# A dilated causal convolution on one core: common parts split a second time in PSUM, and the last 16 channels gathered in DRAM

## The chip, the cores and the metric

One NeuronCore of one Trainium2 chip runs the whole kernel in a single launch. The metric is the device time of one execution in microseconds (us). Engines are named as in the profile: PE is TensorE (PEld its weight loads), ACT is ScalarE, DVE is VectorE, POOL is GpSimd, and SP is the engine that here only issues transfers.

## What is computed

The reference is one WaveNet layer: a causal convolution with 15 taps, dilation 2, 144 channels in and 288 out, a gate, and a projection of 144 by 144.

```
B, T, D, K = 2, 16000, 144, 15          # x: B,T,D   w: K,D,2D   w_o: D,D   (all bf16)
xp = pad(x, 28 zeros in front of T)
h  = sum over i of  xp[:, 28-2i : 28-2i+T, :] @ w[i]
f, g = h[..., :144], h[..., 144:]
return (tanh(f) * sigmoid(g)) @ w_o
```

## The kernel before

**Tiling.** Both sequences and a gap of 32 zero tokens form one line of 32032 tokens. It is cut into ten blocks of 3072 tokens and one of 1536. Even and odd tokens are two planes, so that dilation 2 becomes a step of 1 inside a plane. A block of 3072 has two units (r = 0 and 1), the last block has one: 21 units. In a unit each of 128 rows of a matmul result stands for 12 pairs of output positions.

**Fewer matmuls.** Taps are not multiplied one by one. A Karatsuba-like scheme (L129 and L135 to L183) makes sums and differences of shifted inputs on DVE: S, D, E of the input at a distance of 8, S4, D4, E4 of those at a distance of 4, and Sr, Dr, Er of the last 16 channels. Four parts m = 0 to 3 use (S, D, E, E). Each part has a common product V (`pe_V`, 8 matmuls: two banks of 4) and two private products A for b2 = 1 and 0 (`pe_A`, two banks of 4 matmuls plus 1 for the last 16 channels). A unit has 110 of these matmuls, each 128 by 128 against 288 columns, and from the second unit on 24 of 144 columns for the projection. ACT copies V and A of parts 0 and 1 out of PSUM as bf16 (L291), DVE adds them (L129), for parts 2 and 3 with the A operand read from PSUM. `gate_act` makes tanh and sigmoid on ACT (L306, L307), `gate_mul` their product z on DVE.

**The last 16 channels.** 144 channels do not fit 128 rows. `load_x` transposes channels 0 to 127 into `xn` and channels 16 to 143 into `xb`, two DMA transposes each (L117). `load_r` copies the last 16 rows of `xb` eight times, each shifted by one token, into `rx` (L125, 16 rows by 2 planes by about 1544 tokens each), so that one matmul covers eight taps of those channels.

**Projection and store.** `start_zT` transposes z by DMA (L318), `outproj` multiplies it with `w_o` one unit later (groups of 6 matmuls, ACT copies each group to `os`, L329), `store` writes `os` to the output (L348). In a 64-row store each packet is one token of 288 bytes.

**Order.** Every engine runs in program order, written out by hand and kept (`K_`). SP issues all steady transfers in order: in an odd unit zT, the four transposes of the block after next, the store; in an even unit zT, the eight copies to `rx`, the store. All SP transfers share one DMA queue (q1), ACT's are on q10, POOL's on q0.

**PSUM.** Three two-bank tiles `acc` and two one-bank tiles `po`, all eight banks.

Of the kernel before, what the change touches and what calls it, by code (L numbers as in the profile page):

```python
# [15 lines left out]
def kernel(  # L16
# [6 lines left out]
):  # L23

# [38 lines left out]
    v_pool = ctx.enter_context(tc.tile_pool(name="v", bufs=4))  # L63
# [3 lines left out]
    ps_acc = ctx.enter_context(tc.tile_pool(name="ps_acc", bufs=3, space=bass.MemoryType.PSUM))  # L67
    ps_out = ctx.enter_context(tc.tile_pool(name="ps_out", bufs=2, space=bass.MemoryType.PSUM))
# [34 lines left out]
    blocks = {}  # L103

    def load_x(bi, names=("xn", "xb")):
        loads, zeros = segs(bi)
        cur = blocks.setdefault(bi, dict(bi=bi))
        for nm in names:
            c0 = 0 if nm == "xn" else D - P
            t_ = xa_pool.tile([P, 2, XW], BF16, name=nm)  # L110
            cur[nm] = t_
            for (a, e) in zeros:
                K_(nc.gpsimd.memset(t_[:, :, a:e], 0.0))
            for e in range(2):
                for (col, b, tk, n) in loads:
                    src = bass.AP(x.tensor, x[b, tk + e, c0].offset, [[2 * D, n], [1, P]])
                    K_(nc.sync.dma_start_transpose(out=t_[:, e, col:col + n], in_=src))  # L117

    def load_r(bi, engs=None):
        engs = engs or (nc.sync,)  # L120
        cur = blocks[bi]
        cw = HA + BTOK[bi] // 2
        rx = xa_pool.tile([P, 2, XW], BF16, name="rx")
        for i in range(8):
            K_(engs[i % len(engs)].dma_start(out=rx[CR * i:CR * (i + 1), :, 8:cw], in_=cur["xb"][P - CR:P, :, 8 - i:cw - i]))  # L125
        cur["rx"] = rx

    def tt(out_, a, b, op):
# [4 lines left out]
           "Sr": (0, 8), "Dr": (0, 8), "Er": (-8, 16)}  # L133

    def derive(bi, nm):  # L135
        cur = blocks[bi]
        big = bi < NBIG
        npd = BTOK[bi] // 48
        u0, wd = GEO[nm]
        t_ = d_pool.tile([P, GEO[nm][1] * P], BF16, name=nm)  # L140
        cur[nm] = t_

        def src(x_, u):

            s = u + HA
            v = x_[:, :, s:s + PU * npd]
            if big and wd == PU:
                return v
            return v.rearrange("p e (k j) -> p e k j" if big else "p e (k j) -> p j e k", j=PU)[
                (slice(None),) * (3 if big else 1) + (slice(0, wd),)]  # L150

        if nm in ("S4", "D4", "E4"):
            b = cur[nm[0]]
            bw = GEO[nm[0]][1]
            if big:
                b3 = b[:].rearrange("p (n j) -> p n j", j=bw)
                tt(t_[:].rearrange("p (n j) -> p n j", j=wd), b3[:, :, 4:4 + wd], b3[:, :, 0:wd], ALU.subtract)
            else:
                rw = 2 * npd
                tt(t_[:, 0:wd * rw], b[:, 4 * rw:(4 + wd) * rw], b[:, 0:wd * rw], ALU.subtract)  # L160
            return
        x_ = cur["rx" if nm[-1] == "r" else "xn"]
        if big:
            o = t_[:].rearrange("p (e c) -> p e c", e=2) if wd == PU else \
                t_[:].rearrange("p (e k j) -> p e k j", e=2, j=wd)
        else:
            o = t_[:, 0:wd * 2 * npd].rearrange("p (j e k) -> p j e k", e=2, k=npd)
# [5 lines left out]
    def stat(cur, nm, u):  # L173

        u0, wd = GEO[nm]
        blk, r = cur["blk"], cur["r"]
        t_ = blk[nm]
        if r is None:
            rw = 2 * (BTOK[blk["bi"]] // 48)
            return t_[:, (u - u0) * rw:(u - u0 + 2) * rw]  # L180
        return t_[:].rearrange("p (n j) -> p n j", j=wd)[:, :, u - u0 + r]


    wz = const.tile([P, 512], BF16)
    K_(nc.vector.memset(wz[:], 0.0))
    w_all = const.tile([CM, K, D2], BF16)
    wrA = const.tile([P, D2], BF16)
    wrB = const.tile([P, D2], BF16)
    K_(nc.gpsimd.memset(wrB[96:P, :], 0.0))
    for (t0, t1) in ((0, 4), (4, 8), (8, 12), (12, K)):  # L190
        K_(nc.scalar.dma_start(out=w_all[:, t0:t1, :], in_=w[t0:t1, 0:CM, :].rearrange("k c d -> c k d")))
    warm = const.tile([P, 1], F32)
    K_(nc.gpsimd.memset(warm[:], 0.0))
    K_(nc.scalar.activation(out=warm[:], in_=warm[:], func=ACT.Sigmoid))
    load_x(0)
# [5 lines left out]
    ident = const.tile([P, P], BF16)  # L201
    make_identity(nc, ident[:])
    K_(nc.gpsimd.dma_start(out=wrA[:], in_=w[0:8, CM:D, :]))
    K_(nc.gpsimd.dma_start(out=wrB[0:7 * CR, :], in_=w[8:K, CM:D, :]))
    load_r(0, (nc.sync, nc.gpsimd))
    load_x(1)
# [7 lines left out]
    load_r(1, (nc.sync, nc.gpsimd))  # L214

    wps = ps_acc.tile([P, 2, 512], F32, name="acc")
    for _ in range(54):
        K_(nc.tensor.matmul(wps[:, 0, :], lhsT=wz[:, 0:P], rhs=wz[:], start=True, stop=True))

    G1 = const.tile([CM, 7, D2], BF16)  # L220
    Gm = const.tile([CM, 7, D2], BF16)
    H = const.tile([CM, 4, 4, D2], BF16)
    Wr = const.tile([P, 4, 2, D2], BF16)

    tt(H[:, 2], w_all[:, 0:4, :], w_all[:, 4:8, :], ALU.add)
    GO = ((G1, ALU.add), (Gm, ALU.subtract))
    for (g, op) in GO:
        tt(g[:, 0:4, :], w_all[:, 0:4, :], w_all[:, 8:12, :], op)
    for m, (g, op) in enumerate(GO):
        tt(g[:, 4:7, :], w_all[:, 4:7, :], w_all[:, 12:15, :], op)  # L230
        tt(H[:, m, 0:3, :], g[:, 0:3, :], g[:, 4:7, :], ALU.add)
        tt(H[:, m, 3, :], g[:, 3, :], w_all[:, 7, :], ALU.add)
    derive(0, "S")
    derive(0, "D")
    derive(0, "E")
    tt(H[:, 3, 0:3], w_all[:, 8:11, :], w_all[:, 12:15, :], ALU.add)
    derive(0, "S4")
    tt(Wr[:, 0, 1, :], wrA[:], wrB[:], ALU.add)
    tt(Wr[:, 1, 1, :], wrA[:], wrB[:], ALU.subtract)
    derive(0, "D4")  # L240
    derive(0, "Sr")
    derive(0, "Dr")
    derive(0, "E4")
    derive(0, "Er")
    K_(nc.scalar.copy(out=H[:, 3, 3, :], in_=w_all[:, 11, :]))
    for m in (2, 3):
        K_(nc.scalar.mul(out=Wr[:, m, 0, :], in_=(wrA[:], wrB[:])[m - 2], mul=-1.0))
    front_neg = [lambda m=m: K_(nc.scalar.mul(out=Wr[:, m, 0, :], in_=Wr[:, m, 1, :], mul=-1.0)) for m in range(2)]

    def Gw(m, i):  # L250
        j = i + 8 * (m - 2) if m >= 2 else i
        if m < 2 and i < 7:
            return (G1, Gm)[m][:, i, :]
        return w_all[:, j, :] if j < K else None

    def Rw(m, b2):
        return Wr[:, m, b2, :] if m < 2 or not b2 else (wrA, wrB)[m - 2][:]
# [4 lines left out]
    HALF = (0.5, 0.5, 1.0, 1.0)  # L262

    def mm_bank(ps, jobs):
        n = len(jobs)
        for k, (l, r) in enumerate(jobs):
            K_(nc.tensor.matmul(ps, lhsT=l, rhs=r, start=(k == 0), stop=(k == n - 1)))  # L267

    def pe_V(cur, m):
        acc = ps_acc.tile([P, 2, 512], F32, name="acc")  # L270
        for b1 in range(2):
            mm_bank(acc[:, b1, 0:D2], [(stat(cur, NM[m], SH[m] + 2 * b1 - i), H[:, m, i, :]) for i in range(4)])
        return acc

    def pe_A(cur, m, b2):
        acc = ps_acc.tile([P, 2, 512], F32, name="acc")
        for b1 in range(2):
            jobs = []
            for i in range(4):
                wt = Gw(m, i if b2 else i + 4)  # L280
                if wt is not None:
                    jobs.append((stat(cur, NM[m] + "4", SH[m] + 2 * b1 - i - (0 if b2 else 4)), wt))
            jobs.append((stat(cur, NM[m] + "r", SH[m] + 2 * b1 + 4 * b2), Rw(m, b2)))
            mm_bank(acc[:, b1, 0:D2], jobs)
        return acc
# [4 lines left out]
    def act_ev(dst, acc, sign=1.0):  # L290
        K_(nc.scalar.activation(out=dst, in_=acc[:, :, 0:D2], func=ACT.Copy, scale=sign))  # L291

    def ev_V(acc, m):
        v = v_pool.tile([P, 2, D2], BF16, name="v")
        act_ev(v[:], acc, HALF[m])
        return v

    def bc(v):
        v = v[:]
        return bass.AP(v.tensor, v.offset, [list(v.ap[0]), [0, 2]] + [list(p) for p in v.ap[1:]])  # L300

    def gate_act(cur, c0, n=4):
        th = g_pool.tile([P, 4, D], BF16, name="th")
        sg = g_pool.tile([P, 4, D], BF16, name="sg")
        y = cur["y"]
        K_(nc.scalar.activation(out=th[:, 0:n], in_=y[:, c0:c0 + n, 0:D], func=ACT.Tanh))  # L306
        K_(nc.scalar.activation(out=sg[:, 0:n], in_=y[:, c0:c0 + n, D:D2], func=ACT.Sigmoid))  # L307
        cur["g", c0] = (th, sg, n)

    def gate_mul(cur, c0):  # L310
        th, sg, n = cur["g", c0]
# [4 lines left out]
    def start_zT(cur):  # L316
        zT = zt_pool.tile([P, ZW // P, P], BF16, name="zT")
# [4 lines left out]
    def outproj(cur, g):  # L322
        po = ps_out.tile([P, 512], F32, name="po")
# [214 lines left out]
```

## Time and profile before

| what | value |
|---|---|
| median of 3 runs | 353.64 us (352.66 to 357.31) |
| profiled execution: own time | 354.34 us |
| profiled execution: span from first to last instruction | 352.6 us |
| mean granted TensorE clock | 0.989 |
| busy: PE, PEld, DVE, ACT | 95%, 90%, 83%, 63% |
| DMA | 141881 packets, 45.33 MB; q1 busy 73.6% of 16 engines |

Times in the trace count from the start of the span. A group of the profile is one line of code, engine, operation and shape, with its busy time and the mean of one in ns. An x288 matmul shows some 286 ns because the pipeline is filled and emptied in it; one starts every 0.122 us. The chain of waits follows the work that ended last from the end back to the start. The trace also holds each DMA packet with start, duration, size and queue.

### The profile page before, as it was taken

How to read it: one execution, taken by the hardware profiler on the slowest of the kernel's cores; microseconds unless marked ns; L12 is line 12 of the kernel's file. 1: busy time of each engine (PE TensorE's matmuls, PEld its weight loads, DVE VectorE, ACT ScalarE, POOL GpSimd, SP SyncE). 2: the span in 40 equal slices, each digit the busy share in tenths (PEclk: the TensorE clock that was granted, in tenths of full speed). 3: DMA queues.
4: the chain of work that ended last, by engine and by line, in shares of the span. 5: the costliest groups of instructions: out<-in, count | busy, mean ns of one | idle time of the engine just before them, and what ended most of it. 6: DMA issues, size and time to landing. Idle time of an engine off the chain costs nothing.

```text
span 352.6 us, 7171 instructions
## 1 busy us (share of the span) xinstructions
PE 334.4 (95%) x2891; PEld 318.0 (90%) x2892; DVE 293.2 (83%) x393; ACT 220.8 (63%) x388; POOL 21.3 (6%) x48
## 2 busy tenths in 40 slices
PE   8938899999999999989999999989999999999994
PEld 3527799999999999989999999989999999999873
DVE  1826999789889888977988897878889889979984
ACT  2122567576765767657576765757676575776773
POOL 5255100000000000000000000000000000000002
PEclk9987999999999999999999999999999999999999
DMA  9998899969869787697997888698789865633224
GB/s 203 132 119 181 89 157 148 120 131 180 129 97 196 145 91 145 110 162 110 196 151 94 161 122 137 86 187 168 92 169 159 121 116 90 121 73 60 59 46 93
DMA packets 141881, 45.33 MB, mean 129 GB/s; under 512 B 136938, under 2 KB 139306, under 8 KB 141848
## 3 DMA queue, kind: packets, MB, share of 16 engines
q1 hardware_dynamic: 138588, 42.28, 73.6%
q0 software_dynamic: 1024, 1.43, 3.1%
q10 hardware_dynamic: 2236, 1.17, 1.3%
q8 instruction: 22, 0.36, 0.4%
q14 instruction: 11, 0.09, 0.1%
HBM read 1.62 MB, written 9.22 MB: 31 GB/s over the span
## 4 chain that ended last, share of the span: by engine, by line
PE 83%; DMA 9%; SPq 3%; DVE 2%; POOL 1%; ACT 1%; issue 0%; ACTq 0%; POOLq 0%
PE acc L267 74%; PE po L267 9%; DMA zT<-z 6%; SPq L117 3%; DMA wo_ab<-in_w_o_dram 2%; DMA xb<-in_x_dram 1%; DVE y L129 1%; POOL rx L125 1%; DVE m L129 0%; POOL wo_ab L211 0%; POOL wo_ab L212 0%; PE acc L359 0%; DVE mm L129 0%; DVE u L129 0%; DVE Sr L129 0%
## 5 line engine op out<-in xcount | busy, mean ns | idle before, releaser
L267 PEld LDWEIGHTS <-E 128*128 128x128 bf16 x966 | 117.5, 144 | 2.8 <-issue 1.8
L267 PE MATMUL acc<-w_all,E 128*128 128x288 bf16 x630 | 101.3, 286 | 1.7 <-DVE y L129 1.7
L329 ACT CAST os<-po 128x432 bf16<-128x432 f32 x80 | 41.4, 517 | 59.6 <-PE po L267 59.5
L267 PEld LDWEIGHTS <-S 128*128 128x128 bf16 x504 | 62.7, 142 | 1.6
L291 ACT ACTIVATE v<-acc 128x576 bf16<-128x576 f32 x84 | 52.4, 649 | 18.4 <-PE acc L267 18.4
L267 PEld LDWEIGHTS <-D 128*128 128x128 bf16 x504 | 63.2, 141 | 0.6
L267 PE MATMUL acc<-G,S 128*128 128x288 bf16 x294 | 49.4, 291 | 0.0
L267 PE MATMUL acc<-Gm,D 128*128 128x288 bf16 x294 | 48.0, 286 | 0.0
L306 ACT ACTIVATE th<-y 128x576 bf16<-128x576 bf16 (+1 forms) x64 | 43.4, 678 | 4.9 <-DVE y L129 4.9
L267 PE MATMUL po<-wo_ab,zT 128*128 128x144 bf16 x480 | 43.1, 226 | 3.2 <-DMA zT<-z 3.2
L267 PE MATMUL acc<-H,E 128*128 128x288 bf16 x336 | 44.6, 286 | 0.0
L307 ACT ACTIVATE sg<-y 128x576 bf16<-128x576 bf16 (+1 forms) x64 | 43.0, 672 | 0.0
L291 ACT ACTIVATE mm<-acc 128x576 bf16<-128x576 f32 x42 | 27.4, 652 | 24.1 <-PE acc L267 24.1
L267 PEld LDWEIGHTS <-zT 128*128 128x128 bf16 x480 | 35.3, 98 | 6.2 <-DMA zT<-z 4.3
L129 DVE TENSOR_TENSOR y<-m,acc 128x576 bf16<-128x576 bf16 x42 | 31.3, 752 | 8.5 <-PE acc L267 8.1
L129 DVE TENSOR_TENSOR m<-m,v 128x1152 bf16<-128x1152 bf16 x42 | 31.7, 755 | 3.6 <-ACT m L291 1.5
L129 DVE TENSOR_TENSOR z<-th,sg 128x576 bf16<-128x576 bf16 (+1 forms) x64 | 28.8, 449 | 6.3 <-ACT sg L307 5.3
L291 ACT ACTIVATE m<-acc 128x576 bf16<-128x576 f32 x42 | 26.9, 654 | 9.5 <-PE acc L267 9.5
L129 DVE TENSOR_TENSOR y<-u,acc 128x576 bf16<-128x576 bf16 x42 | 31.4, 748 | 0.6 <-PE acc L267 0.5
L267 PE MATMUL acc<-Wr,Sr 128*128 128x288 bf16 x84 | 24.5, 292 | 7.1 <-DVE Sr L129 7.1
L129 DVE TENSOR_TENSOR mm<-mm,v 128x1152 bf16<-128x1152 bf16 x21 | 15.9, 758 | 16.3 <-ACT mm L291 16.2
L267 PEld LDWEIGHTS <-Er 128*128 128x128 bf16 x168 | 24.2, 144 | 0.2
(65 smaller groups left out, 396.3 us busy)
## 6 DMA issues: line engine op xcount, KB each, us to landing
out_dram<-os SPq DMA_DIRECT2D x36, 216.0 KB
rx<-xb SPq DMA_DIRECT2D x72, 96.5 KB
w_all<-in_w_dram ACTq DMA_DIRECT2D x3, 288.0 KB
rx<-xb POOLq DMA_DIRECT2D x8, 96.5 KB, 5.6
out_dram<-os SPq DMA_DIRECT2D x4, 168.8 KB
rx<-xb SPq DMA_DIRECT2D x8, 48.5 KB
xn<-in_x_dram SPq DMA_TRANSPOSE x24
xb<-in_x_dram SPq DMA_TRANSPOSE x24
```

Of the source, the lines that this page charges most:

```text
L117: K_(nc.sync.dma_start_transpose(out=t_[:, e, col:col + n], in_=src))
L125: K_(engs[i % len(engs)].dma_start(out=rx[CR * i:CR * (i + 1), :, 8:cw], in_=cur["xb"][P - CR:P, :, 8 - i:cw - i]))
L129: return K_(nc.vector.tensor_tensor(out=out_, in0=a, in1=b, op=op))
L267: K_(nc.tensor.matmul(ps, lhsT=l, rhs=r, start=(k == 0), stop=(k == n - 1)))
L291: K_(nc.scalar.activation(out=dst, in_=acc[:, :, 0:D2], func=ACT.Copy, scale=sign))
L306: K_(nc.scalar.activation(out=th[:, 0:n], in_=y[:, c0:c0 + n, 0:D], func=ACT.Tanh))
L307: K_(nc.scalar.activation(out=sg[:, 0:n], in_=y[:, c0:c0 + n, D:D2], func=ACT.Sigmoid))
L329: K_(nc.scalar.copy(out=cur["os"][:, 3 * g:3 * g + 3, :].rearrange("p a d -> p (a d)"), in_=po[:, 0:3 * D]))
```

## The change

The common product is split once more. For each part, a first matmul pair (`v_common`) with 2 weights writes bank 0 of a tile X. ACT copies bank 0 to bank 1 inside PSUM (`copy_b1`). PE adds 2 private matmuls to each bank (`v_private`, stationary operands S2, D2, E2, new differences at a distance of 2 made by DVE). ACT copies each bank to a one-bank tile Y (`copy_b2`). PE then adds the private products of b2 = 1 onto X and of b2 = 0 onto Y, without starting a new accumulation. V has 6 matmuls for 8, a unit 102 for 110. V is no longer copied out or added on DVE; two of the four evictions of parts 0 and 1 become halves (`use`). Work is written as 84 periods (21 units by 4 parts), with v_common two periods ahead and v_private one; the projection of a unit is spread over the two units behind it. PSUM is now two X tiles of two banks, three Y and one `po`.

For the last 16 channels, `xb` and its transposes and the eight shifted copies are gone. `gather_r` copies channels 128 to 143 of a block's tokens from x to a DRAM buffer `rs` (runs of 32 bytes); `load_r` reads it by two DMA transposes whose rows overlap: each row has 256 bytes and begins 32 bytes after the one before. At the start, weight sums of parts 2 and 3 are made on PE with an identity matrix and copied out by ACT, and the warm-up is shorter. At the end, the transposes of z are grouped by four.

```diff
-    ps_acc = ... bufs=3 (two banks each)     ps_out = ... bufs=2
+    ps_x = ... bufs=2 (two banks each)   ps_y = ... bufs=3   ps_o = ... bufs=1
+    def gather_r(bi, eng):
+        for (col, b, tk, n) in segs(bi)[0]:
+            src = bass.AP(x.tensor, x[b, tk, CM].offset, [[D, 2], [2 * D, n], [1, CR]])
+            K_(eng.dma_start(out=bass.AP(rs[bi].tensor, rs[bi][col, 0].offset, [[RW[bi] * CR, 2], [CR, n], [1, CR]]), in_=src))
     def load_r(bi):
-        for i in range(8):
-            K_(engs[i % len(engs)].dma_start(out=rx[CR * i:CR * (i + 1), :, 8:cw], in_=cur["xb"][P - CR:P, :, 8 - i:cw - i]))
+        for e in range(2):
+            src = bass.AP(rs[bi].tensor, rs[bi][e * n + 1, 0].offset, [[CR, n], [1, P]])
+            K_(nc.sync.dma_start_transpose(out=t_[:, e, 0:n], in_=src))
...
+    gather_r(0, nc.scalar)          # behind the four loads of w_all
+    load_x(0)
+    load_r(0)
...
+    gather_r(1, nc.sync)
+    load_x(1)
+    load_r(1)
...
     def pe_V(cur, m):
-        acc = ps_acc.tile([P, 2, 512], F32, name="acc")
-        for b1 in range(2):
-            mm_bank(acc[:, b1, 0:D2], [(stat(cur, NM[m], SH[m] + 2 * b1 - i), H[:, m, i, :]) for i in range(4)])
+        mm(ps[:, 0, 0:D2], [(stat(cur, NM[m], SH[m] - j), H[:, m, 4 + j, :]) for j in range(2)], True)
+    def pe_Vp(cur, ps, m, b1):
+        mm(ps[:, b1, 0:D2], [... 2 jobs of NM[m] + "2" ...], False)
+    def copy_b1(q):
+            K_(nc.scalar.copy(out=X[q][:, 1, 0:D2], in_=X[q][:, 0, 0:D2]))
+    def copy_b2(q, b1):
+            Y[q, b1] = y_bank()
+            K_(nc.scalar.copy(out=Y[q, b1][:, 0:D2], in_=X[q][:, b1, 0:D2]))
+    def use(q, b2, b1=None):
+        if m < 2:   # ACT: scaled(..., 0.5), 576 columns of X or 288 of Y
+        else:       # DVE: tt(y, P, X or Y), 576 or 288 columns
+    def loads(ui, k):
+        if r == 1 and k == 2 and bi + 2 < NBLK:
             load_x(bi + 2)
+            gather_r(bi + 2, nc.sync)
+        if r == 0 and k == 2 and 1 <= bi and bi + 1 < NBLK:
             load_r(bi + 1)
+    def period(q):
+        if m == 0:
+            gate_act(p1, 0, 0); fill(ui, "E", "S"); gate_mul(p1, 8)
+            fill(ui, "E2", "S2", "S4", "D"); ... derive(bi, "Dr") ...; fill(ui, "E4")
+        if m == 1:
+            gate_mul(p1, 0); start_zT(p1)
...
+        pe_A(cur, X[q][:, 0, 0:D2], m, 1, 0, part)
+        pe_A(cur, X[q][:, 1, 0:D2], m, 1, 1, part)
+        v_private(q + 1)
+        use(q, 1)
+        copy_b2(q + 1, 0)
+        if m == 1:
+            both(cur, 1); fill(ui, "Er", "Sr")
...
+        pe_A(cur, Y[q, 0][:, 0:D2], m, 0, 0, part)
+        use(q, 0, 0)
+        copy_b2(q + 1, 1)
...
+        pe_A(cur, Y[q, 1][:, 0:D2], m, 0, 1, part)
+        use(q, 0, 1)
...
+        if m == 3 and p1 and not last:
+            outproj(p1, 0)
+        elif m < 3 and p2:
+            outproj(p2, m + 1)
+        v_common(q + 2)
+        copy_b1(q + 2)
+        if m == 2 and p2:
+            store(p2)
+        loads(ui, m)
```

Here p1 and p2 are the units one and two before the present one, and `segs(bi)[0]` gives one run of n = 1552 even and 1552 odd tokens for a full block (1536 for the first, 672 for the last, two shorter runs for the block in which the first sequence ends).

## The prediction

> **What bounds the kernel now.** I read the page first, then the chain of waits, then the stages of single units and SP's timeline. The page:
>
> ```profile
> PE 334.4 (95%) x2891; PEld 318.0 (90%) x2892; DVE 293.2 (83%) x393; ACT 220.8 (63%) x388; POOL 21.3 (6%) x48
> ...
> PE acc L267 74%; PE po L267 9%; DMA zT<-z 6%; SPq L117 3%; DMA wo_ab<-in_w_o_dram 2%; DMA xb<-in_x_dram 1%; DVE y L129 1%; POOL rx L125 1%; DVE m L129 0%; POOL wo_ab L211 0%; POOL wo_ab L212 0%; PE acc L359 0%; DVE mm L129 0%; DVE u L129 0%; DVE Sr L129 0%
> ```
>
> The convolution's matmuls carry three quarters of the chain. Busy times in two units of the middle (start:end, length, then each engine, clock, DMA share, GB/s):
>
> ```profile
> 115.22:130.22 15.00, 15.00 (x137) 14.90 (x135) 12.65 (x17) 10.27 (x18) 0.25 (x2) 1.00 0.83 126
> 238.35:253.34 14.99, 14.99 (x137) 14.89 (x135) 12.64 (x17) 10.27 (x18) 0.00 (x0) 1.00 0.88 138
> ```
>
> PE has no gap in a unit of 14.99 us. Ten such matmuls in the chain take 1.23 us, so 0.1225 each; 110 of them and 24 small ones at 0.06 (0.38 for 6) make the 14.99. DVE has 2.3 us of room, ACT 4.7. The DMA engines are at 83 to 88%. They do hold PE up where a transpose of z comes late; the chain there, and SP's timeline:
>
> ```profile
> 206.41 5.74 PE acc L267 x47
> 212.15 4.82 DMA zT<-z
> ...
> 217.01 0.55 PE po L267 x6
> ```
>
> ```profile
> 206.99 5.04 SPq L348 DMA_DIRECT2D out_dram<-os  x6
> 212.15 3.08 SPq L318 DMA_TRANSPOSE zT<-z  x1
> ```
>
> zT stood in SP's queue behind six stores, landed after 4.8 us and PE waited for it at the projection: what is in front on q1 decides when zT lands. Units 2 to 19 run from 55.25 to 328.32 in the chain, 273.1 us, 3.3 of them such stalls (18 x 14.99 = 269.8). The first two units end at 55.25, the last with the end takes 24.2.
>
> **The matmuls.** 8 of 110 go: 14.99 - 8 x 0.1225 = 14.01 us per unit, 252.2 for 18 units.
>
> **ScalarE.** Per unit 6 of 8 evictions of 576 columns go (0.65 each, 3.9), 4 halves and 12 bank-to-bank copies of 288 come. The nearest row is the 288-column copy out of PSUM:
>
> ```profile
> L373 ACT CAST os<-po 128x288 bf16<-128x288 f32 x5 | 2.0, 400 | 1.5 <-PE po L267 1.5
> ```
>
> No row has PSUM as destination; bounds are 0.325 (half of the 576 eviction) and 0.65 (all of it). At 0.40: 10.27 - 3.9 + 6.4 = 12.8 of 14.01, hidden under PE. It passes 14.01 at 0.48 a copy; at 0.65 a unit would be 16.8.
>
> **VectorE.** Six 1152-wide additions go (6 x 0.757), four 576-wide come (0.45 each); of the four 0.75 reads of PSUM two become four halves (0.45, the copy of 288 at L375); S2, D2 (0.56 each, the row of 768 elements) and E2 (0.95, that of 1536) come per two units, 1.03 a unit. Net -4.5 + 1.8 + 0.3 + 1.0 = -1.4: hidden. New waits: PE now waits for ACT's copies before v_private, A on X and A on Y. Laying one period of 3.55 us out by these durations, copy_b1 ends 0.8 us into the period that needs it at 1.2, copy_b2 0.3 us before its period begins. I cost these at nothing; the cover is thin, and 0.3 us a unit would be 6 us.
>
> **The last 16 channels.** Gone: per block eight copies of 256 packets of 3088 bytes, 443 ns each by the packet records, 7 us of all 16 engines, and 5.6 us of SP issues. The transposes stay four. POOL issues 17 more small writes of zeros (0.53 us each by its rows, 9 us) ahead of w_o, which PE first needs after 60 us: nothing. New is one gather: 3104 packets of 32 bytes, DRAM to DRAM. Two questions price it.
>
> On how many DMA engines? In the packet records the stores differ by shape. A 64-row store has 12 to 18 packets in flight. The 50-row store at 212 us has exactly 10, one per engine and 20.8 ns each (480 packets per us):
>
> ```profile
> 212.00:213.00 1.00, 1.00 (x11) 1.00 (x9) 0.65 (x1) 0.65 (x1) 0.00 (x0) 1.00 0.64 139
> ```
>
> 0.64 of 16 is 10, the largest number up to 16 that divides 50. The 4-byte packets that end a transfer's share agree over the whole run: q1 has 4204, which is 32 for each of 68 transposes, 16 for each of 80 copies and 36 stores, and for the odd stores 10 (50 rows), 13, 9 (27 rows), 14 (28) and 4 (one row of four runs), 4 of each and 2 with 28. The slowest dimension of the gather counts 2. By the same pattern it runs on two engines, 1552 packets on each. The Trainium skill says so in DMA: Bandwidth & Descriptors, section "Why a DMA increments its semaphore by 16 and not by 1": the engines used are the largest number up to 16 that divides the slowest dimension above 1 of both sides. The trace agrees with its 4204; no run here shows it between two DRAM buffers.
>
> How long is a packet? Rows: 4 bytes 9.2 ns, 32 bytes on q0 15.1, 288 bytes 20.8. I take 15.1, the same size: 23.4 us for a gather, with ends 14.3 and 32.3. The same page (section "Measured (HBM→SBUF, 128 partitions, SWDGE, issued from GpSimd)") has about 10.5 ns for a packet in a tiny transfer; by that estimate the sum below would be some 414.
>
> **Where it lies.** Count from the start of an odd unit. The store waits for the third period's projection, 11.3, and takes 1.3; two transposes of xn 3.6 (1.8 each); the gather's packets begin 1 us later, at 17.2, and end at 40.6. SP itself is held for 0.7 us (the issue of a copy now) or, if an issue lasts as long as its packets wait, for all of it; either way everything that SP issues next queues behind it on those two engines: zT of the next unit (issued near 20), its store, then load_r, which waits for the gather itself. zT's own 1792 packets take 2.2 us (244.2 to 246.4): landed at 42.8. PE needs it for outproj(p1, 0) at the end of the fourth period of the even unit, 14.0 + 13.3 = 27.3. Stall 15.5 us. A PE that idles that long is slowed afterwards: after its 7.1 us wait at 20 us in this trace the matmuls of 27.4 to 30.8 come every 0.24 us, 1.7 us lost. So 17.2 per block; SP, ACT, DVE and the next gather all shift with it, so it repeats. Seven blocks (3 to 9): 120.4. Block 2, whose gather comes earlier in its unit: 12.7. The last block (672 packets per engine, 10.1 us): 2.2. Together 135.
>
> Start: the first gather follows w_all on ACT's queue (its packets end near 9): 9 + 23.4 + 0.8 = 33.2; two transposes 4.8; Sr 0.7: 38.7, against 26.67 + 0.7 now. PE has then done 24 of unit 0's 102 matmuls; 78 x 0.1225 + 1.7 gives 50. Block 1's gather goes out behind load_r(0): 38 to 61.4, and xn(1) behind it lands at 64. DVE needs xn(1) for S in unit 1 and has 8.1 us queued there (S 1.22, S2, S4 0.95, D 1.22, both, Sr, gate products, use) before the X tile is free that PE wants at 60.5; it gets it at 72.1. Stall 11.6 + 1.7. Unit 1 ends at 50 + 14.0 + 13.3 = 77.3 (now 55.25). The weight sums on PE and ACT at the start lie before 38.7 and cost nothing, even if ACT is held by its gather until 33.
>
> End: 24.2 - 0.98 - 0.8 (zT's wait at 337) = 22.5; the three projections moved behind the last unit are the same work.
>
> Sum: 77.3 + 252.2 + 135 + 22.5 = 487.0 of span; 1.74 us lie around it in the profiled execution (354.34 against 352.6), whose time is 0.70 above the median: 488. With 14.3 per gather the same steps give 57.4 + 252.2 + 60 + 22.5 + 1.0 = 393; with 32.3, 95 + 252.2 + 211.5 + 22.5 + 1.0 = 582.
>
> **Rivals.** (1) The gather is spread over 16 engines, so the change pays. At the rate at which the 64-row store's packets start (580 per us) 3104 take 5.4 us, over at 22.6; zT lands by 25, before 27.3. No stall. At the start rx lands near 17 and DVE's sums and differences set the end of unit 0, about 32, so unit 1 ends at 46: 46 + 252.2 + 22.5 + 1.0 = 322; with 0.1 us of waits a unit 324. For it: no DRAM-to-DRAM copy is in the trace. Against: six shapes that all follow the divisor. (2) Two engines but packets near 7 ns, the shortest of the 4-byte ones: the gather 10.9, stall 3.0 a block, some 24 in all and 6 at the start: 322 + 30 = 352, no change. This is also the point from which (1) decides: below 7 ns faster, above slower; with 5.3 ns no stall is left. Against: no packet with data is under 13 ns. (3) ScalarE takes over. At 0.65 a copy, 2.8 us a unit on 20 units, 56 on top of 324: 380. With one copy per 0.55 us: 346. For it: in-order waits on PE and 28 instructions a unit. Against: 0.40 for the same columns out of PSUM. It would ride on (1), and hides under the stalls of my forecast.
>
> **How the numbers follow.** Two engines and packets of 9 to 21 ns, 393 to 582: 0.74, at its middle row 488, the prediction. ScalarE as the bound without the gather, some 380: 0.03. No measurable change, 346 to 361: 0.05. The change pays, near 324: 0.18. A difference of 2% is what a measurement of this kernel can tell from none, so faster 0.18, same 0.05, slower 0.77. The range from 346 to 582 holds the middle and the slower cases, 0.8 in all; it leaves out rival (1). The forecast's own range is 393 to 582.
>
> **What would show it.** Right: 32-byte packets with at most two or so in flight for 20 us and more per block; a DMA share near 2 of 16 in those stretches; PE waiting for zT or for DVE's Sr once per block, 10 us and more, with the granted clock down after it; units between the stalls of 14.0 us. Wrong: a gather over within 6 us (engines), packets far from 15 ns (price), units longer than 14.3 us with ACT over 95% busy (rival 3), or a first unit that is over by 33 us. A forecast that is off by a few us per block but has the stalls in their place is a mis-sized packet, not another mechanism.

## The result, and the profile after

The changed kernel takes 455.94 us (median of 4 runs, 454.44 to 458.05), the kernel before 353.83 in the same session: a ratio of 1.287, 95% interval 1.277 to 1.297. The profiled execution took 454.44 with a span of 452.7 and a mean granted clock of 0.878. Its page, busy times first, then the chain by engine and by line:

```profile
PE 336.4 (74%) x2738; PEld 306.4 (68%) x2739; DVE 263.6 (58%) x433; ACT 267.7 (59%) x604; POOL 27.0 (6%) x56
...
PE 44%; DMA 36%; DVE 7%; SPq 5%; ACT 2%; POOL 2%; issue 1%; DVEq 0%; POOLq 0%; ACTq 0%
DMA zT<-z 32%; PE px L267 27%; PE py L267 12%; PE po L267 5%; SPq L135 4%; DVE y L148 3%; DMA wo_ab<-in_w_o_dram 2%; DMA wr_f<-in_w_dram 1%; DVE D L148 1%; POOL rs L123 1%; DVE S L148 1%; ACT py L454 1%; DMA xn<-in_x_dram 1%; DVE E L148 1%;
```

PE has 153 matmuls fewer and is busy for 74% of the span instead of 95%. The transposes of z, 6% of the chain before, are 32% of it now. The table of PE's waits (line, what it waited for, us in all, times, longest) says how often:

```profile
PE po L267 <- DMA zT<-z: 82.3, 8, 13.5
PE px L267 <- DVE Sr L148: 14.7, 1, 14.7
PE px L267 <- DVE y L148: 3.4, 1, 3.4
```

There are eight waits for zT, one behind the gather of each block from 2 to 9, and one at the start for Sr, which needs the first gather. One of the eight in the chain, and SP's issues around it:

```profile
108.88 1.97 PE px L267 x16
110.85 0.11 PE py L267
110.96 18.61 DMA zT<-z
129.57 0.04 issue
129.62 0.90 PE po L267 x6
```

```profile
103.61 4.05 SPq L135 DMA_TRANSPOSE xn<-in_x_dram  x2
107.70 0.69 SPq L118 DMA_DIRECT2D rs<-in_x_dram  x1
110.96 16.82 SPq L367 DMA_TRANSPOSE zT<-z  x1
127.87 1.25 SPq L397 DMA_DIRECT2D out_dram<-os  x2
129.21 4.37 SPq L145 DMA_TRANSPOSE rx<-rs  x2
```

The gather (L118) is issued in 0.69 us; the transpose of z behind it holds SP for 16.82 and lands at 129.6. What the DMA engines do meanwhile, in 40 equal slices of 108 to 129 us (the time of the packets in flight as a share of 16 engines, in tenths, then GB/s):

```profile
DMA  9498132222222222222222222222222222279299
GB/s 158 62 280 163 11 40 8 6 5 5 5 5 6 5 5 5 5 5 5 5 5 5 5 5 5 5 5 5 5 6 5 5 6 5 5 103 145 33 286 290
```

For 16 us the share is about a quarter and 5 GB/s pass, which is the gather alone; then zT goes at up to 290. By the packet records the gather's 3104 packets take 16.9 us (109.9 to 126.8), with 3.75 in flight, 20.4 ns each; 3.75 of 16 is the quarter. None of zT's 256-byte packets starts before 126.5, on any engine, though SP began to issue it at 110.96: zT does not share two engines with the gather, it waits as a whole. Around the gather, unit by unit (start:end, length, PE, PEld, DVE, ACT, POOL, clock, DMA share, GB/s):

```profile
89.60:105.40 15.80, 15.70 (x127) 14.46 (x126) 7.77 (x16) 12.33 (x29) 0.00 (x0) 0.90 0.65 113
105.40:130.79 25.39, 14.86 (x126) 14.22 (x126) 15.75 (x23) 12.49 (x29) 0.00 (x0) 0.85 0.53 68
130.79:146.46 15.67, 15.58 (x127) 14.42 (x126) 7.76 (x16) 12.32 (x29) 0.00 (x0) 0.91 0.66 115
410.18:424.19 14.01, 14.01 (x126) 13.73 (x126) 10.34 (x20) 12.30 (x29) 0.00 (x0) 1.00 0.46 87
```

The unit without a gather near it takes the 14.01 us forecast. The even unit takes 25.4, and the odd units beside it 15.7 to 15.8 at a clock of 0.90: the clock falls to half 4.3 us after PE has gone idle and comes back about 4 us after it has resumed, in the next unit. In all seven waits of 10 us and more it falls after 3.5 to 4.3 us and comes back after 2.6 to 4.3; its records change in steps of 3.41 us.

### The profile page after: what moved, and what is told of

It is laid out like the page before. It is cut to its first block, busy times and chain, and to the rows that moved or that the text cites. A ratio compares the mean times of both kernels' runs of the same rounds, so it can differ in the third digit from the quotient of the medians.

```text
span 452.7 us, 7007 instructions
## 1 busy us (share of the span) xinstructions
PE 336.4 (74%) x2738; PEld 306.4 (68%) x2739; DVE 263.6 (58%) x433; ACT 267.7 (59%) x604; POOL 27.0 (6%) x56
## 4 chain that ended last, share of the span: by engine, by line
PE 44%; DMA 36%; DVE 7%; SPq 5%; ACT 2%; POOL 2%; issue 1%; DVEq 0%; POOLq 0%; ACTq 0%
DMA zT<-z 32%; PE px L267 27%; PE py L267 12%; PE po L267 5%; SPq L135 4%; DVE y L148 3%; DMA wo_ab<-in_w_o_dram 2%; DMA wr_f<-in_w_dram 1%; DVE D L148 1%; POOL rs L123 1%; DVE S L148 1%; ACT py L454 1%; DMA xn<-in_x_dram 1%; DVE E L148 1%; DVE z L148 1%
## 5 line engine op out<-in xcount | busy, mean ns | idle before, releaser
L267 PE MATMUL po<-wo_ab,zT 128*128 128x144 bf16 x480 | 46.0, 236 | 83.9 <-DMA zT<-z 82.3
L454 ACT COPY py<-px 128x288 f32<-128x288 f32 x168 | 65.1, 388 | 24.6 <-DVE y L148 14.9
L267 PE MATMUL px<-w_all,E 128*128 128x288 bf16 x336 | 54.2, 288 | 1.1 <-ACT py L454 0.8
L352 ACT ACTIVATE th<-y 128x576 bf16<-128x576 bf16 (+1 forms) x64 | 43.4, 678 | 13.2 <-DVE y L148 13.2
L267 PE MATMUL py<-WN,E 128*128 128x288 bf16 x294 | 48.6, 288 | 0.0
L267 PE MATMUL px<-H,E 128*128 128x288 bf16 x252 | 45.3, 289 | 0.0
L148 DVE TENSOR_TENSOR y<-P,py 128x288 bf16<-128x288 bf16 x84 | 37.2, 453 | 13.4 <-PE py L267 13.0
L457 ACT ACTIVATE m<-px 128x576 bf16<-128x576 f32 x42 | 27.4, 651 | 29.5 <-PE px L267 28.3
L148 DVE TENSOR_TENSOR y<-P,px 128x576 bf16<-128x576 bf16 x42 | 31.7, 754 | 19.9 <-PE px L267 19.8
L457 ACT ACTIVATE m<-py 128x288 bf16<-128x288 f32 x84 | 34.8, 414 | 6.5 <-PE py L267 1.3
L443 ACT COPY px<-px 128x288 f32<-128x288 f32 x84 | 34.9, 415 | 4.1 <-PE px L267 4.1
L267 PE MATMUL px<-G,S 128*128 128x288 bf16 x168 | 34.5, 344 | 2.1 <-ACT py L454 1.4
L267 PE MATMUL px<-G,D 128*128 128x288 bf16 x168 | 27.6, 293 | 0.3 <-ACT py L454 0.3
```

Source lines behind the costliest of these rows:

```text
L148: return K_(nc.vector.tensor_tensor(out=out_, in0=a, in1=b, op=op))
L267: K_(nc.tensor.matmul(ps, lhsT=l, rhs=r, start=start and k == 0, stop=stop and k == n - 1, skip_group_check=not start))
L352: K_(nc.scalar.activation(out=cur["g", c0][k][:, 0:n], in_=cur["y"][:, c0:c0 + n, D * k:D * k + D], func=(ACT.Tanh, ACT.Sigmoid)[k]))
L443: K_(nc.scalar.copy(out=X[q][:, 1, 0:D2], in_=X[q][:, 0, 0:D2]))
L454: K_(nc.scalar.copy(out=Y[q, b1][:, 0:D2], in_=X[q][:, b1, 0:D2]))
L457: K_(nc.scalar.activation(out=dst, in_=ps, func=ACT.Copy, scale=0.5))
```

## The experiments

The theory: two engines carry the gather, and zT queues behind it. The rivals: the order of SP's queue alone, the mere number of short packets, or the new convolution. The kernel before ran beside each run on the same chip: at 352.9 us beside runs 1 to 3 and the first of run 6, 354.1 beside 4, 5, 7 and the second of run 6, 354.5 beside 8. Ratios are to these; two times from different groups can differ by 1 to 2 us for that alone.

**1. Tokens outermost.** The same 3104 packets, in an order whose slowest dimension counts the tokens (1552 = 16 x 97), not the 2 planes.

```diff
-src [[D, 2], [2 * D, n], [1, CR]]      dst [[RW[bi] * CR, 2], [CR, n], [1, CR]]
+src [[2 * D, n], [D, 2], [1, CR]]      dst [[CR, n], [RW[bi] * CR, 2], [1, CR]]
```

> The changed kernel with the two outer dimensions of the gather exchanged: tokens outermost (1552), planes inside (2). Same bytes, same 32-byte packets, same place in every queue. Two-engines theory: 16 engines, 3104 packets in 5.4 us or less (the 580 packets per us of a 64-row store) for 16.9; no wait for zT at the projection, units of 14.0 us; first unit over near 33; 320 to 332 us. Rival, 32-byte packets from DRAM to DRAM are slow wherever they run (184 per us in total): still 17 us a gather and about 455. Rival, the waits on ScalarE cost the time: no change, about 455.

Measured: 339.83 us, ratio 0.962 (0.958 to 0.965): faster than the kernel before, though 8 us above the expected range. A gather of 3104 packets on SP's queue now lasts 1.6 to 2.8 us with 10 to 19 packets in flight of 9.0 to 9.6 ns. The 4-byte packets, one for each engine's share of a copy, are 3004 on q1: 16 for each of its 11 gathers, where the changed kernel's 2850 had 2. The slices of 110 to 117 us of this run, the gather among them at 57 to 90 GB/s:

```profile
DMA  9999889897999999999999830005999990000029
GB/s 287 290 285 197 105 98 143 151 116 142 291 287 291 288 206 90 57 68 61 73 75 82 43 18 4 0 0 117 183 203 203 111 15 0 6 9 10 9 50 278
```

No wait for zT is left, in the same queue order. So the 116 us between the two kernels hang on which dimension stands first. Against my estimate three things are late: unit 2 begins at 51.24 (46 expected), 18 units take 258.5 (252.2), the end 29.1 (22.5).

**2. The gather on ACT's queue.** Two planes outermost as in the change, but the steady gathers are issued by ACT, so zT does not stand behind them.

```diff
-            gather_r(bi + 2, nc.sync)
+            gather_r(bi + 2, nc.scalar)
```

> The changed kernel with the gathers of blocks 2 to 10 issued by ScalarE instead of SP, at the same place in the program; still two engines. Two-engines theory with its second half, that zT stands behind the gather in the same queue: zT now only shares two engines, lands within some 5 us, and what is left is load_r, which waits for the gather on SP with the next zT behind it: 350 to 400 us. Rival, the length of the gather itself (rx comes late) sets the period, whichever queue it is on: above 440. Rival, 32-byte packets disturb every DMA: above 440.

Measured: 411.26, ratio 1.165 (1.162 to 1.169), between the two expectations, a miss for both. Of the eight waits for zT one is left (10.0 us), and another kind takes their place:

```profile
DVE Sr L148 <- DMA rx<-rs: 50.7, 8, 12.2
```

The steady gathers now take 20 to 23 us with some 2 packets in flight, beside the stores and transposes of SP's queue, and `load_r`, which needs the gather whole, brings rx too late. Taking zT out from behind the gather is worth some 45 us; the gather's length does harm on its own. Whether the other traffic or ACT's queue itself slows the gather, no run separates.

**3. Split in two copies, meant for four engines.**

```diff
+for e in range(2):   # one copy for each plane
+    src [[2 * D * (n // 4), 4], [2 * D, n // 4], [1, CR]]
```

> The changed kernel with each gather as two DMAs, one per plane, whose slowest dimension is 4 (388 tokens each): 776 packets on each of four engines. Two-engines theory: 776 at 10.9 ns is 8.5 us for 16.9; the stall of 10.9 us per block shrinks by 8.4 to 2.5 and is too short to lower the clock; the start is some 15 us shorter; about 360 us (350 to 372). Rival, a total rate of 184 packets per us: 455. Rival, two transfers cost more than one: above 455.

Measured: 340.34, ratio 0.965 (0.964 to 0.967). It says nothing about four engines: the 4-byte packets count 3180, 16 for each of 22 copies, and a gather is over in 2.2 us. The two outer dimensions, whose strides run on evenly, must have become one of 1552. The run is of use all the same: it has two copies for one on 16 engines, units 2 to 19 in 258.4 us, and the start of unit 2 at 51.98.

**4 and 5. Four and eight engines.** Strides that do not run on: the slowest dimension takes every k-th token.

```diff
+m = n // k           # k = 4, then 8
+for e in range(2):
+    src [[2 * D, k], [2 * D * k, m], [1, CR]]      dst [[CR, k], [CR * k, m], [1, CR]]
```

> The gather as two copies, one for each plane, whose slowest dimension counts 4 (tokens j, j+4, j+8, ... for j = 0 to 3). Theory (the time goes with the number of engines): 776 packets on each of four engines; at the 10.9 ns of the changed kernel 8.5 us a gather; it begins about 18.5 us after an odd unit's start, ends near 27, zT lands 2 to 3 us later, and PE wants it near 27.8: a stall of some 2 us in each of 8 blocks, 16 in all, and about 5 at the start on top of the 340 of the token-outer gather: 360, range 350 to 372. The 4-byte packets of q1 should count 2916 (2828 + 22 x 4). Rival (the order of the packets or their addresses, not the engines, made the token-outer gather short): near 340, as there, or near 456, as the changed kernel.

> The same with a slowest dimension of 8: 388 packets on each of eight engines, 4.2 us a gather, over 23 us after the odd unit's start and zT landed by 26, before PE wants it: no stall for zT. Theory: 338 to 346, with 3004 4-byte packets on q1. Rival (order or addresses): the same time as with 4, whatever that is.

Measured: 364.92, ratio 1.028 (1.022 to 1.034), and 344.98, ratio 0.972 (0.965 to 0.978), both inside the expected ranges; the 4-byte packets count 2916 and 3004 as foreseen. With the changed kernel and run 1:

| slowest dimension | packets per engine | steady gather, us | us per packet and engine | units 2 to 19, us | time, us |
|---|---|---|---|---|---|
| 2 (the change) | 1552 | 16.9 | 0.0109 | 354.3 | 455.9 |
| 4 | 776 | 7.8 | 0.0101 | 276.2 | 364.9 |
| 8 | 388 | 3.6 | 0.0093 | 258.3 | 345.0 |
| 1552, so 16 | 194 | 1.8 | 0.0093 | 258.5 | 339.8 |

The length goes as one over the number of engines, and the units stop paying once the gather is over before zT is wanted. Run 3 shows that two copies in place of one cost the units nothing. PE's table for four engines:

```profile
PE po L271 <- DMA zT<-z: 11.8, 7, 2.8
```

The 5.2 us by which eight engines stay behind sixteen (4.6 between the spans of the profiled executions) lie at the start, not in the loop: the issue of the second of the two copies on ACT's queue holds ACT to 11.0 us, when the first copy is nearly through (11.6), and ACT has the first sums of weights to copy out. ACT's first gather with eight engines, then with sixteen:

```profile
3.12 7.88 ACTq L122 DMA_DIRECT2D rs<-in_x_dram  x2
```

```profile
2.96 0.80 ACTq L118 DMA_DIRECT2D rs<-in_x_dram  x1
```

Unit 2 begins at 56.37 instead of 51.24, 5.1 us later. With four engines it is 10.1 us of ACT, and 59.35; with two copies on 16 engines (run 3) 4.9 us of ACT, and only 51.98. So it is the length of the gather, more than the number of copies, that costs the start.

**6. The new convolution with the old copies.** `xb` and the eight shifted copies stay (with one buffer for `xb`, m0 and m1 to fit); only the PSUM half is made.

> Only the PSUM part of the change: the last 16 channels come as before, from a transposed xb and eight shifted copies (in reversed order, one buffer for xb and for the two halves m, for lack of memory). No gather. Two-engines theory: units of 14.0 us, a few waits for zT as before (3 to 5 us in all), first two units over near 53, end 28: 333 to 345 us, faster than before. Rival, ScalarE's bank-to-bank copies hold PE up: units above 14.5, no faster than 350.

Measured: 371.67, ratio 1.053 (1.048 to 1.058): a miss. DVE's table:

```profile
DVE Sr L138 <- DMA rx<-xb: 27.2, 7, 7.4
```

The copies are issued at the end of the third period here, mostly 12.6 us into the even unit, where the kernel before has them 6.0 to 9.6 us into it. Moved right behind zT, which puts them at 7 to 13 us (5 expected):

```diff
         start_zT(p1)
+        if r == 0 and 1 <= bi and bi + 1 < NBLK:
+            load_r(bi + 1)
```

> The new convolution with the old xb and eight shifted copies, the copies issued right behind zT in the second period of the even unit in place of the end of the third. Theory (in the run with the copies kept, 371.67, only their lateness cost): the copies are issued from about 5 us into the unit, land by 18, and Sr is wanted near 19 to 20: no wait of DVE for rx, 338 to 350. Rival (the eight copies cost the shorter unit more than their lateness, by DMA traffic in front of zT or by SP's issues): 358 to 372, with waits for zT or DVE's Sr still above 15 us.

Measured: 343.60, ratio 0.969 (0.963 to 0.975); the wait falls to 4.5 us, 2 times. The PSUM half pays alone, if the copies leave early.

**7. The gather without the new convolution.** The kernel before, its last 16 channels by the 16-engine gather and two overlapping transposes (the weights of those channels put in the order of the new rows).

> The kernel before with only the second half of the change, and the gather in token-outer order: convolution in PSUM as before (110 matmuls a unit), last 16 channels by gather and two overlapping transposes. Theory (the transfers are hidden when the gather is over in 2 us, and a unit is bound by its matmuls): units stay at 15.0 us, only the 3.3 us of waits for zT can go and the start can move by a few us: 345 to 354. Rival (the transfers themselves pay): under 342; (the gather or the overlapping transposes disturb even so): over 358.

Measured: 345.73, ratio 0.974 (0.968 to 0.979). Where the gain comes from is in the chain, here the end of unit 1 and the start of unit 2, then the end of unit 19:

```profile
45.73 0.38 PE po L289 x6
46.10 10.05 PE acc L289 x82
56.15 0.38 PE po L289 x6
```

```profile
316.39 0.99 PE acc L289 x8
317.38 0.38 PE po L289 x6
317.76 5.05 PE acc L289 x42
```

Unit 2 begins at 46.10 where it began at 55.25: 9.15 of the 9.3 us of span. Units 2 to 19 take 271.7 (273.1 before), 15 us each as ever, and the end gives back 1.2. So the gain lies at the start, because rx no longer waits for `xb` and eight copies: PE's wait of 7.1 us for Sr is gone.

**8. Retimed.** Run 1, with DVE's order and `load_r` moved.

```diff
-            load_r(bi + 1)  at k == 2                        +            load_r(bi + 1)  at k == 1
-        m == 1: both(cur, 1); fill(ui, "Er", "Sr")           +        m == 1: fill(ui, "Er"); both(cur, 1); fill(ui, "Sr")
-        m == 3: fill(ui, "D2")  ahead of use(q, 0, 0)        +        m == 3: fill(ui, "D2")  behind use(q, 0, 1)
+        units[ui] == (NBIG - 1, 0): derive(NBIG, "E") at m == 3
+        units[ui] == (NBIG - 1, 1): derive(NBIG, "E2"), "Dr" at m == 0, "Er" at m == 3
```

> The token-outer gather, with DVE's work in another order and rx loaded one period earlier: Er before the sums of parts 0 and 1 in the second period, D2 behind the last use of the fourth, and E, E2, Dr and Er of the last, small block in the two units before it. In the token-outer run PE waits in its loop for Er (11 times, 2.8 us) and ACT's copies to Y behind DVE (2.5), once for rx (2.3), and at the start of the last unit the chain has E 2.80, Dr 0.97 and Er 1.87 of DVE alone. Theory (these are late only by their place in DVE's queue): 3 to 5 us in the loop and 4 to 5 at the end, 339.8 to about 331, range 328 to 335. Rival (DVE's queue has no room there, so the waits come back elsewhere): 336 to 341.

> The token-outer gather once more, beside the retimed version on one chip. Both theories: 338 to 341, as before.

Measured on one chip: 335.96, ratio 0.947 (0.944 to 0.950), and 340.25, ratio 0.959 (0.956 to 0.962). The gain of 4.3 us is half of the 9 expected: a miss for the theory (328 to 335), at the edge of what its rival said (336 to 341), that DVE has no room there and the waits come back elsewhere. In run 1 the last unit began with DVE alone, in the chain:

```profile
309.30 0.45 DVE y L148
309.75 2.80 DVE E L148
312.55 0.36 DVE z L148
312.91 0.47 DVE E L148
313.38 0.97 DVE Dr L148
```

That is gone, but the same work now delays the two units before it (14.75 and 15.51 us instead of 14.71 and 14.02); the end is 27.8 where it was 29.1. In the loop the one wait for rx (2.3 us, in unit 13) is gone, and an odd unit takes 14.02 instead of 14.27, an even one 14.20 instead of 14.16. What D2 had cost the odd units is in the chain of run 1, at the end of one:

```profile
134.38 0.75 DVE y L148
135.13 0.56 DVE D L148
135.69 0.37 DVE y L148
136.06 0.02 issue
136.09 0.39 ACT py L454
```

The difference (D, the name without its number) stood between two uses of a part, and ACT's copy to Y waited for the second of them to free a bank. It is the fastest of all the kernels, 5% under the kernel before.

## Why the prediction was right, step by step

**Engines: right, and shown.** The slowest dimension of 2 put the gather on two engines. The table above varies only that number (and, for 4 and 8, has two copies for one, which run 3 clears), and length and time follow. The Trainium skill's rule (DMA: Bandwidth & Descriptors, section "Why a DMA increments its semaphore by 16 and not by 1"), which the trace before showed only on other shapes, agrees with these DRAM-to-DRAM copies for 2, 4, 8 and 16: 2850, 2916, 3004 and 3004 4-byte packets (the last two are 22 x 8 and 11 x 16). Rival (1), a spread over 16 engines whatever the shape, falls; as a mechanism it was the right one for run 1.

**Packet: mis-sized.** I took 15.1 ns for one after the other on an engine, from the 32-byte packets of POOL's queue; 16.9 us over 1552 is 10.9. A record lasts 20.4, but about two overlap on each engine, which that row could not show: there 34 packets are spread over 1.7 us, 0.3 in flight. The gather is 16.9 us for 23.4, within my ends of 14.3 and 32.3. The Trainium skill (DMA: Bandwidth & Descriptors, section "Measured (HBM→SBUF, 128 partitions, SWDGE, issued from GpSimd)") has its 10.5 ns from the shortest transfer's 0.67 us over its 64 packets, which is not the pace of one engine; that it lies near 10.9 shows nothing. The estimate of 414 that I drew from it is 42 too low, for the reasons below.

**Stall in a block: the place right, the size 13 for 17.2.** The gather begins 20.3 us after the odd unit's start, not 17.2. The store goes 1.4 us later, since that unit is itself slowed by the half clock of the one before (15.8 for 14.0); the two transposes take 4.05 us for 3.6; and the gather's first packet comes 2.2 us after its issue begins, where I had 1. It ends at 37.2 (40.6 forecast), zT lands at 40.0 (42.8), PE wants it at 29.5 (27.3). Waits for zT are 82.3 us: 4.9 for block 2 (11.0 forecast) and 10.2 to 13.5 for the seven others (15.5). The last block, for which I had 2.2, costs nothing: its gather is over in 6.6 us. The half clock costs some 2.0 per stall (1.7), and 0.4 per block is a loss of the new convolution that run 1 has as well (28.43 for 28.02). Together the stalls and these losses are 102.1 over 18 units, where I had 135. SP's issues lie between the two ways that I left open: the gather's is short, and the next one lasts for the whole gather. I had zT queue behind the gather "on those two engines"; in the trace it does not start on any. Why the other engines do not begin with it, no run shows.

**Start: Sr done at 35.8 (38.7), unit 0 at an end at 50.3 (50), unit 1 at 69.9 (77.3).** The first gather is shorter (18.5 us), but the rest of unit 0 takes 14.5 us for the 11.3 I gave it: PE runs 86 matmuls there where I counted 78 (eight are the first of unit 1), and the clock is at half for the first 5.7 us, 2.8 lost for 1.7. The shorter second gather lets xn of block 1 land at 56.1 (64), so PE waits 3.4 where I had 11.6.

**End: 28.5 for 22.5.** I took the same work for the same time. But DVE's E, Dr and Er of the small last block now stand alone in the chain, 2.79, 0.97 and 1.87 us (run 1's first two are shown under run 8); my sum had no term for them.

**The sum.** 69.9 + 252.2 + 102.1 + 28.5 = 452.7, against 77.3 + 252.2 + 135 + 22.5 = 487. With 10.9 ns in my own steps the sum would have been about 421, an estimate: the long packet put 66 us too much into the forecast, and the delays that I left out (start, late gather, end, the 0.2 us a unit) some 32 too little. That 488 came within 7% is partly luck, since these errors have opposite signs; that the stalls lie where they were forecast is not.

**The rest.** The one unit with neither a stall nor the half clock in it is 14.01 us, as computed. ScalarE's bank-to-bank copies, priced at 400 ns, by form (busy, mean ns):

```profile
L454 ACT COPY py<-px 128x288 f32<-128x288 f32 x168 | 65.1, 388 | 24.6 <-DVE y L148 14.9 <-PE px L267 5.2
L443 ACT COPY px<-px 128x288 f32<-128x288 f32 x84 | 34.9, 415 | 4.1 <-PE px L267 4.1
```

ACT needs 12.3 us a unit (12.8 forecast) and never sets the pace: rival (3) falls. But the copies to Y wait for DVE, 14.9 us in all, and that is the cover which I called thin: with PE's waits for Er it makes most units 14.16 or 14.27 in run 1, with a last even one of 14.7: some 4 us over 18 units that "at nothing" left out.

**Where the expected gain went.** With a short gather the two halves give little more together (339.8) than each alone (343.6 and 345.7). By spans: the gather half brings the start 9.15 us forward. On top of it the new convolution saves 13.2 in units 2 to 19 (271.7 to 258.5) and gives back 5.1 at the start (51.24 for 46.10), where everything is a chain of PE, ACT and DVE, and 3.5 at the end (29.1 for 25.5). What causes those two losses in detail was tried only for the end, in run 8.

## What to carry to other kernels

Look at the slowest dimension of a DMA with short runs before anything else: here the exchange of two dimensions in one access pattern is worth 116 us, and the count of 4-byte packets that close each transfer says afterwards how many engines were used. Here the transfer that is long on few engines harms most by what is queued behind it, and next by who needs it whole, so shortening it (116 us) is worth more than moving it to another queue (45). When the loop of a tuned kernel gets shorter, cost its start and its end anew: here 5.1 and 3.5 us of the gain were lost to chains there that nothing covers.

## What the runs showed that I had not expected

The gather's pace on two engines is not constant: in each of the steady gathers of 3104 packets 285 to 328 packets start in the first us, and from the third us on some 170 per us. Taken over all of it, and counting two engines by the closing packets, that is 10.9 ns per packet and engine, with about two records of 20.4 ns overlapping; on 16 engines a record is 9.0 to 9.6 ns.

On two engines a gather on a second queue takes 20 to 23 us beside other traffic, for 16.9. A copy's issue takes 0.6 to 1.3 us however long the copy runs; the next issue in that engine's order pays, 16.8 us for zT, and two gathers in a row held ACT for 4.9 (16 engines), 7.9 (8) and 10.1 (4). Two dimensions with strides that run on evenly seem to count as one: the split meant for 4 engines closed 16 shares.
